# An attention and feed-forward kernel on one core: from sixteen chunks of 288 tokens to nine of 512

## The chip, the cores and the metric

The kernel runs on one core of a Trainium2 chip. The core has a matrix engine (TensorE, PE in the profile; PEld is its loading of weights), a vector engine (VectorE, DVE), a scalar engine (ScalarE, ACT), GpSimd (POOL) and a synchronisation engine (SyncE, SP), which here issues all data transfers. The engines run at the same time, each through its own queue in order, and wait for each other by semaphores. The metric is the device time of one execution in microseconds (us). Three runs of the kernel before took 929.86, 930.31 and 932.52 us; the median is 930.31.

## The reference

```python
# q, k, v: (8, 8, 576, 64) fp32: batch, heads, sequence, head width
window, dilation = 32, 4
scores = q @ k.T / sqrt(64)
rel = pos[:, None] - pos[None, :]
mask_plain = (rel >= 0) & (rel < window)                                        # heads 0 to 3
mask_dil = (rel >= 0) & (rel < window * dilation) & (rel % dilation == 0)       # heads 4 to 7
attn = softmax(where(mask, scores, -1e9))
x = (attn @ v) as (4608 tokens, 512)
out = gelu(x @ w_in) @ w_out              # w_in (512, 2048), w_out (2048, 512)
```

Each query sees at most 32 keys, near ones in the plain heads and every fourth position in the dilated ones. The feed-forward part is two dense products over 4,608 tokens.

## The kernel before, in words

**The products.** Every feed-forward operand is kept as two parts in a short format (`F32R`), a high one and a low one, and a product is made as three: high by high, low weight by high, high weight by low. In the first layer (`ffn_h`, the loop of products at L506) a block `f` of 128 of the 2,048 hidden units takes 4 blocks of inputs by 3, so 12 products; in the second layer (`ffn_o`, L520) each of 4 output blocks `d` takes 16 blocks `f` by 3. That is 16 x 12 + 4 x 16 x 3 = 384 products for one chunk of tokens. Each product has 128 x 128 weights, loaded by an instruction of its own, and streams the chunk's tokens as its columns.

**The chunks.** A chunk is half a batch element: 288 tokens, 16 chunks, 16 x 384 = 6,144 products of 288 columns. After a first-layer block, ACT applies gelu (L510) and makes the high part (L513), and DVE subtracts to get the low one (L515). All of the first layer of a chunk stands before its second layer. The second layer goes output block by output block, and each result is copied (L188, L186) and stored (L545).

**The attention.** The four pairs of heads of a chunk are worked in blocks of 32 queries by 64 keys. Scores (L338) and weighted sums (L458, in the first two chunks L442) are fp32 products on parts of the matrix engine. A chunk has 9 blocks a plain head and 12 or 8 a dilated one, so 84 or 68 products of each kind. Between them DVE adds masks and takes the extreme (L350, L365, L370), ACT does the exponentials (L377), DVE or POOL normalises (L398 to L407), DVE turns the blocks (L417, L422), and ACT and DVE split the result into the two parts of x (L492, L495).

**The weights.** They come as fp64 bit patterns (two 32-bit words a number) and are split into the two parts on the chip: DVE operations at L206 to L231 and L241, one ACT copy at L218. For some, a second load shifted by two bytes (`mid`, L198) saves one DVE operation. After this first stage the weights stay in the core's memory.

**What sets the order.** The first stage (chunks 0 and 1 whole, the attention of chunk 2, all weights) is ordered by a small planner, `Plan`: each job names its steps with an engine and an assumed cost, the buffers it takes from named rings, and a rank; the planner always takes the job that can start first. From chunk 2 on the order is a table: attention steps of chunk c stand at fixed places among the products of chunk c - 1 (`A_SC` for scores, `A_X` for weighted sums, and others). Every engine then does its instructions strictly in the order in which they were recorded, the transfers on SP too.

## Time and profile before

| what | before |
|---|---|
| time, median of 3 runs | 930.31 us (929.86 to 932.52) |
| span of the profiled execution, first to last instruction | 927.7 us |
| instructions in the span | 26,396 |
| PE busy | 900.7 us, 97% |
| DVE, ACT, POOL busy | 492.9, 425.4, 13.1 us |
| mean granted clock of the matrix engine | 1.000 |

For the profiled execution the trace holds its span alone; the median of the runs is 2.6 us above it, and that difference is used as what lies around a span. A group of the profile names the line, the engine, the operation, the tile written and the tiles read, the shape, the count, the busy time, the mean duration in ns, and the idle time ahead of it with what ended it. In the chain of waits a row is the start, the length, the engine, the tile and the line. In the timeline a row is the start, the length to the end of the last instruction merged in it, and the instructions. An fp32 product appears as two records; some records of products are missing.

### The profile page before, as it was taken

The numbers are of one execution on the slowest core, as the hardware profiler recorded it, in microseconds if no ns is written. First come the engines' busy times: TensorE is split into PE (matmuls) and PEld (weight loads), VectorE is DVE, ScalarE is ACT, GpSimd is POOL, SyncE is SP. The second block draws the span as 40 slices with busy tenths as digits, with TensorE's granted clock in tenths as the row PEclk, the third lists the DMA queues.
The fourth block names the chain that finished last, engine by engine and source line by source line (L and its number), as shares of the span: only waits on it lengthen the run. The fifth ranks groups of instructions, "written<-read, shape, count | busy, mean of one in ns | idle before, by whom it ended". The sixth has DMA issues, their size and how long they took to land.

```text
span 927.7 us, 26396 instructions
## 1 busy us (share of the span) xinstructions
PE 900.7 (97%) x11120; PEld 887.8 (96%) x11120; DVE 492.9 (53%) x1815; ACT 425.4 (46%) x1365; POOL 13.1 (1%) x39
## 2 busy tenths in 40 slices
PE   3699999999999999999999999999999999999998
PEld 2599999999999999999999999999999999999998
DVE  7899984454625447353463635436363454635420
ACT  4645443624536245353635437254463624536240
POOL 1400000000000000000000000000000000000000
PEclk9999999999999999999999999999999999999999
DMA  9986334013030210303013030211303012020000
GB/s 326 401 318 232 114 107 151 28 38 115 20 133 17 76 61 27 126 24 116 14 39 114 31 122 19 77 58 37 116 20 116 19 50 103 27 82 7 21 1 26
DMA packets 34838, 81.90 MB, mean 88 GB/s; under 512 B 3872, under 2 KB 12064, under 8 KB 34720
## 3 DMA queue, kind: packets, MB, share of 16 engines
q1 hardware_dynamic: 34720, 80.22, 25.3%
q8 instruction: 87, 1.43, 0.7%
q14 instruction: 31, 0.25, 0.1%
HBM read 70.77 MB, written 9.44 MB: 86 GB/s over the span
## 4 chain that ended last, share of the span: by engine, by line
PE 94%; DMA 3%; DVE 1%; POOL 1%; SPq 0%; issue 0%; POOLq 0%; ACT 0%; DVEq 0%
PE ps_o L520 44%; PE ps_h L506 44%; PE px_a L458 3%; PE ps_a L338 2%; DMA raw_w<-w_out 1%; POOL sm L404 1%; DMA raw_w<-w_in 1%; DMA v_sb<-v_d 1%; DMA v_all<-v_d 0%; PE px L458 0%; DVE cv L208 0%; DVE raw_w L225 0%; DVE x L495 0%; DVE sm L365 0%; DVE cv L206 0%
## 5 line engine op out<-in xcount | busy, mean ns | idle before, releaser
L520 PE MATMUL ps_o<-g,wout 128*128 128x288 f32 x3072 | 418.1, 295 | 0.2 <-DVE x L495 0.2
L520 PEld LDWEIGHTS ps_o<-g,wout 128*128 128x128 f32 x3072 | 409.5, 188 | 1.2 <-DVE x L495 0.5
L506 PE MATMUL ps_h<-xh,win 128*128 128x288 f32 x1920 | 387.1, 297 | 0.0
L506 PEld LDWEIGHTS ps_h<-xh,win 128*128 128x128 f32 x1920 | 308.5, 188 | 1.9 <-issue 0.2
L506 PE MATMUL ps_h<-xl,win 128*128 128x288 f32 x960 | 284.0, 296 | 0.0
L515 DVE TENSOR_TENSOR g<-gf,g 128x288 fp32r<-128x288 f32 x256 | 117.1, 457 | 256.3 <-ACT g L513 256.2
L510 ACT ACTIVATE gf<-ps_h 128x288 f32<-128x288 f32 x256 | 105.4, 412 | 282.7 <-PE ps_h L506 282.7
L506 PEld LDWEIGHTS ps_h<-xl,win 128*128 128x128 f32 x960 | 180.8, 188 | 0.0
L513 ACT CAST g<-gf 128x288 fp32r<-128x288 f32 x256 | 111.0, 434 | 7.9
L377 ACT ACTIVATE sm<-sm,st 128x64 f32<-128x64 f32 (+2 forms) x328 | 109.4, 335 | 10.3 <-DVE st L370 9.4
L492 ACT CAST xh<-px_a 128x256 fp32r<-128x256 f32 (+2 forms) x78 | 27.5, 388 | 123.9 <-PE px_a L458 104.3
L422 DVE STREAM_TRANSPOSE turned<-sm 32x128 f32<-32x128 f32 (+2 forms) x248 | 77.5, 313 | 6.2
L188 DVE COPY o_sb<-ps_o 128x288 f32<-128x288 f32 x59 | 26.8, 456 | 79.9 <-PE ps_o L520 78.1
L377 ACT ACTIVATION_READ_ACCUMULATOR sm<-sm,st 128x1 f32 (+2 forms) x328 | 61.2, 187 | 0.0
L495 DVE TENSOR_TENSOR xl<-px_a,xh 128x256 fp32r<-128x256 f32 (+2 forms) x78 | 28.6, 395 | 39.9 <-ACT xh L492 39.8
L350 DVE CUSTOM_DVE_ANT_0 sm<-ps_a,masks 128x64 f32<-128x64 f32 (+1 forms) x284 | 48.2, 218 | 0.6
L417 DVE STREAM_TRANSPOSE turned<-sm 128x256 f32<-128x256 f32 (+2 forms) x90 | 38.9, 432 | 4.4 <-POOL sm L404 1.4
L407 DVE TENSOR_TENSOR sm<-sm,st 128x256 f32<-128x256 f32 (+2 forms) x86 | 35.3, 411 | 2.7
L458 PEld LDWEIGHTS px_a<-turned,v_all 64*64 64x64 f32 x1960 | 30.5, 135 | 2.8 <-issue 2.8
L458 PE MATMUL px_a<-turned,v_all 64*64 64x32 f32 (+1 forms) x1960 | 32.3, 218 | 0.0
L398 DVE TENSOR_SCALAR st<-st 128x4 f32<-128x4 f32 (+2 forms) x90 | 14.4, 160 | 31.5 <-ACT sm L377 30.4
L506 PE MATMUL ps_h<-x,win 128*128 128x288 f32 x192 | 28.1, 295 | 0.0
(46 smaller groups left out, 366.1 us busy)
## 6 DMA issues: line engine op xcount, KB each, us to landing
v_all<-v_p SPq DMA_DIRECT2D x28, 384.0 KB, 4.6
v_all<-v_d SPq DMA_DIRECT2D x28, 384.0 KB, 6.0
raw_qk<-qk_p SPq DMA_DIRECT2D x32, 304.0 KB, 5.1
outT<-o_sb SPq DMA_DIRECT2D x64, 144.0 KB, 1.7
raw_w<-w_in SPq DMA_DIRECT2D x16, 512.0 KB, 6.2
raw_w<-w_out SPq DMA_DIRECT2D x16, 512.0 KB, 6.7
raw_qk<-qk_w SPq DMA_DIRECT2D x16, 384.0 KB, 3.8
mid_w<-w_in SPq DMA_DIRECT2D x9, 511.5 KB, 6.5
```

The lines of the kernel that those rows point to most:

```text
L350: nc.vector.tensor_tensor_reduce(out=s.sm[rs, i], in0=s.sc[h][rs, cols], in1=mask_of(s, u), scale=-SCALE, scalar=3.0e38, op0=ALU.add, op1= ...
L377: nc.scalar.activation(t, t, AF.Exp, bias=s.st[rs, 0, i:i + 1], scale=-1.0, accum_out=s.st[rs, 1, i:i + 1])
L407: nc.vector.tensor_mul(t, t, st.unsqueeze(2).broadcast_to((rs.stop - rs.start, 2 * (u1 - u0), 2 * KB)))
L417: nc.vector.transpose(s.t[rs, i].rearrange("p i j b -> p (i j b)"), s.sm[rs, i].rearrange("p i k -> p (i k)"))
L422: nc.vector.transpose(s.t[32 * to:32 * to + 32, i, r % 2], s.sm[32 * r:32 * r + 32, i, j * KB:(j + 1) * KB])
L458: nc.tensor.matmul(px[h * D:(h + 1) * D, r - r0, u * KB:u * KB + b], s.v[rows, u, j, h * D:(h + 1) * D], s.t[rows, 2 * u + h, j, 0:b], sta ...
L495: nc.vector.tensor_sub(l, y, h)
L506: nc.tensor.matmul(ps, wins[f][:, t, cc * P:(cc + 1) * P], xx, start=(n == 0), stop=(n == 3 * NC - 1))
L510: nc.scalar.activation(gf, ps, AF.Gelu)
L513: nc.scalar.copy(g[:, 0], gf)
L515: nc.vector.tensor_sub(g[:, 1], gf, g[:, 0])
L520: nc.tensor.matmul(ps, wouts[f][:, t, d * P:(d + 1) * P], gs[f][:, u], start=(f == 0 and n == 0), stop=(f == NF - 1 and n == 2))
```

## The change

- A chunk is now 512 tokens: the first 512 of each batch element make chunks 0 to 7, the last 64 of all eight make chunk 8. So 9 x 384 = 3,456 products of 512 columns.
- A chunk's products stand in four phases: first layer of blocks 0 to 7, second layer of these (block by block, all four output blocks in turn), first layer of blocks 8 to 15, second layer of these (output block by output block). The eight accumulator banks are one tile: banks 0 to 3 hold the second layer's sums, banks 4 and 5 the first layer's, and attention borrows 0 to 3 for scores and 4 to 7 for weighted sums.
- From chunk 1 on the next chunk's attention comes in two visits: all scores after the second first-layer block, all weighted sums nine products into the last phase. Chunk 8's dilated heads have queries with 96 keys each and a third visit.
- Scores and masks of a pair are handled by one DVE operation over both heads and one for the extreme. Normalising, turning and splitting are one operation each of 512 columns, and four more turns.
- The first stage holds chunk 0's feed-forward part and the attention of chunks 0 and 1. Their masks are added by TensorE: an identity times the masks starts each accumulation (L296). Chunk 1's probabilities are normalised on ACT and turned on TensorE (L399), and its weighted sums (L413) take 64 keys at once.
- The two layers' weights of a block are loaded together (1 MB), split by operations of 1,024 columns and kept in one ring of 19 tiles, which also takes queries, keys and values. Output copies are on ACT.
- The planner's costs, ranks and the order of first loads are new.

```diff
+N = 512
+NCH = B + 1
+NW_SPARE = 3
+TWICE = (1, 2, 4, 7, 11, 12, 15)
-    wpool = ctx.enter_context(tc.tile_pool(name="wpool", bufs=1))
-    wo = ctx.enter_context(tc.tile_pool(name="wo", bufs=NF + 2))
+    wpool = ctx.enter_context(tc.tile_pool(name="wpool", bufs=NF + NW_SPARE))
+    xg = ctx.enter_context(tc.tile_pool(name="xg", bufs=12))
...
+    def w_split(s, f, cols):
+        low, top, t = s["raw"][:, cols, 0], s["raw"][:, cols, 1], spare["t"][:, cols]
...
+        if f in TWICE:
+            nc.vector.tensor_scalar(low, s["mid"][:, cols], 0x01FFFFFF, None, op0=ALU.bitwise_and)
+        else:
+            nc.vector.tensor_scalar(low, low, 9, None, op0=ALU.logical_shift_right)
+            yield {"DVE": two}
+            nc.vector.scalar_tensor_tensor(low, top, 23, low, op0=ALU.logical_shift_left, op1=ALU.bitwise_or)
...
+        if s.c < 2:
+            for h in range(2):
+                nc.tensor.matmul(s.sc[:, h, s.at:s.at + 2 * P], diag,
+                                 maskr[:, 0 if s.plain else NU:NU if s.plain else 2 * NU].rearrange("p u k -> p (u k)"),
+                                 start=True, stop=False)
...
+    def ffn_h(c, f, gs):
+        yield {"PE": 2.73}
+        bank = ps[:, 4 + f % 2]
...
+    A_SC, A_LOW, A_E, A_N, A_X, A_QK, A_V = 2, 2.5, 8.5, 10.5, 24.75, 26.5, 3
...
+    half = NF // 2
+    for c in range(1, NCH):
+        gs = {}
+        base = 2 * NF * c
+        for f in range(half):
+            at_once(ffn_h(c, f, gs))
+            upto(base + f + 1)
+        for f in range(half):
+            for d in range(NC):
+                ffn_o(d, f, gs)
+                upto(base + half + f + (d + 1) / 4)
+        for f in range(half, NF):
+            at_once(ffn_h(c, f, gs))
+            upto(base + half + f + 1)
+        for d in range(NC):
+            for f in range(half, NF):
+                ffn_o(d, f, gs)
+                upto(base + 3 * half + 2 * d + (f - half + 1) / 4)
+            at_once(store(c, d, 2 if c == LAST and d == NC - 1 else 1))
```

The order on PE before, from the second layer of a late chunk into the first layer of the next one; `ps_o` and `ps_h` are the accumulators of the two layers, `px_a` the weighted sums:

```order
L520 MATMUL ps_o<-g,wout 128x288 x135
L458 MATMUL px_a<-turned,v_all 64x32 x84
L520 MATMUL ps_o<-g,wout 128x288 x57
L506 MATMUL ps_h<-xh,win_121 128x288 x2
L506 MATMUL ps_h<-xl,win_121 128x288
L506 MATMUL ps_h<-xh,win_121 128x288 x2
```

And now, one whole middle chunk; all accumulators are `ps`, L501 and L516 are the two layers, L310 the scores, L459 the weighted sums:

```order
L501 MATMUL ps<-x,weight 128x512 x24
L310 MATMUL ps<-raw_qk 32x64 x128
L501 MATMUL ps<-x,weight 128x512 x72
L516 MATMUL ps<-g,weight 128x512 x96
L501 MATMUL ps<-x,weight 128x512 x96
L516 MATMUL ps<-g,weight 128x512 x9
L459 MATMUL ps<-turned,v_sb 64x32 x128
L516 MATMUL ps<-g,weight 128x512 x87
```

The products have 512 columns in place of 288, a visit has 128 attention products in place of 84 or 68, and there are two visits in 384 products of the longer kind.

The order on SP before, from the last weight to the first loads for the attention of chunk 3, by way of the stores of chunks 0 and 1:

```order
L194 DMA raw_w<-w_out 128x1024
L545 DMA outT<-o_sb 128x288 x3
L286 DMA v_all<-v_p 128x768
L545 DMA outT<-o_sb 128x288
L286 DMA v_all<-v_p 128x768
L286 DMA v_all<-v_d 128x768
L545 DMA outT<-o_sb 128x288
L286 DMA v_all<-v_d 128x768
L545 DMA outT<-o_sb 128x288 x3
L279 DMA raw_qk<-qk_p 128x608 x2
```

And now, from the last weight to the loads for the attention of chunk 2 (with what each waits for), by way of the four stores of chunk 0:

```order
L194 DMA raw_w_1369<-w 128x2048 [waits DMAHW4_49,DVE_49]
L534 DMA outT<-o_sb_1555 128x512 [waits Activation_49]
L534 DMA outT<-o_sb_1557 128x512 [waits DVE_49]
L534 DMA outT<-o_sb_1559 128x512 [waits DMAHW5_49,Activation_49]
L534 DMA outT<-o_sb_1563 128x512 [waits DMAHW6_49,Activation_49]
L260 DMA raw_qk_1657<-qk 128x1024 [waits DMAHW7_49]
L260 DMA raw_qk_1657<-qk 128x1024 [waits DMAHW0_49]
L260 DMA raw_qk_1660<-qk 128x1024 [waits DMAHW1_49]
L260 DMA raw_qk_1660<-qk 128x1024 [waits DMAHW2_49]
L272 DMA v_sb_1829<-v 128x2048 [waits DMAHW3_49]
```

Before, the values for chunk 2's weighted sums were woven among the stores and chunk 2's scores were long done; now all four stores stand ahead of the queries and keys for chunk 2's scores.

## The prediction

> **What bounds the kernel now.** I read the head of the page first, then the chain of waits in order of time, then the matrix engine's timeline near its first product.

> ```profile
> span 927.7 us, 26396 instructions
> PE 900.7 (97%) x11120; PEld 887.8 (96%) x11120; DVE 492.9 (53%) x1815; ACT 425.4 (46%) x1365; POOL 13.1 (1%) x39
> PE   3699999999999999999999999999999999999998
> DVE  7899984454625447353463635436363454635420
> PE 94%; DMA 3%; DVE 1%; POOL 1%; SPq 0%; issue 0%; POOLq 0%; ACT 0%; DVEq 0%
> ```

> PE is busy from the third slice to the last and is 94% of the chain that ends last. Nothing else comes near, so a change is worth what it does to PE's queue, plus what it does to the first 150 us, where PE still waits. The chain shows both:

> ```profile
> 127.65 6.36 PE ps_o L520 x48
> 134.85 4.50 DMA v_all<-v_d
> 139.49 0.90 PE px L458 x48
> ...
> 151.62 6.37 PE ps_h L506 x48
> ...
> 329.93 1.90 PE ps_a L338 x115
> 331.83 14.54 PE ps_h L506 x108
> 346.37 17.88 PE ps_o L520 x135
> 364.25 2.58 PE px_a L458 x168
> 366.83 7.73 PE ps_o L520 x57
> 374.56 6.38 PE ps_h L506 x48
> 380.94 1.58 PE ps_a L338 x97
> ...
> 419.71 2.10 PE px_a L458 x136
> ...
> 899.02 25.43 PE ps_o L520 x192
> ```

> A feed-forward product of 288 columns takes a slot of 25.43/192 = 0.1324 us. The two attention visits of a chunk take 1.90 + 2.58 us (84 products each) or 1.58 + 2.10 us (68 each), so 22.9 ns a score product and 30.8 ns a weighted-sum product; an fp32 product is recorded twice, and some score records are missing, so I count products by the program. After a visit PE needs a little longer: 57 products in 7.73 us are 0.18 us over 57 slots, 108 in 14.54 are 0.24 over, so 0.42 us for a chunk's two visits.

> Check on before: chunk 2's first product is at 151.62; 14 chunks of 384 slots are 711.8 us, 13 chunks' visits 52.7, their restarts 5.5: 921.6. The last copy, quoted below, starts at 924.47. The missing 2.9 us are the four chunks whose visits are split further. The sum can be trusted to half a per cent.

> **The products' length, the largest term.** Both kernels do 4,608 tokens, so the columns streamed are the same: 16 x 384 = 6,144 products of 288 before, 9 x 384 = 3,456 of 512 after. Only what a product costs beside its columns can be saved. The trace has no 512-column product, but it has the 288-column one at two speeds:

> ```profile
> 36.16 0.85 PE L506 MATMUL ps_h<-xh,win 128*128 128x288 f32 x2
> 36.81 0.44 PE L506 MATMUL ps_h<-xl,win 128*128 128x288 f32 x1
> 37.05 0.68 PE L506 MATMUL ps_h<-xh,win 128*128 128x288 f32 x2
> 37.53 0.44 PE L506 MATMUL ps_h<-xl,win 128*128 128x288 f32 x1
> 37.77 0.68 PE L506 MATMUL ps_h<-xh,win 128*128 128x288 f32 x2
> ...
> 41.24 0.43 PE L506 MATMUL ps_h<-xh,win 128*128 128x288 f32 x2
> 41.51 0.29 PE L506 MATMUL ps_h<-xl,win 128*128 128x288 f32 x1
> 41.65 0.43 PE L506 MATMUL ps_h<-xh,win 128*128 128x288 f32 x2
> ```

> Three products are 0.72 us apart at 37 us (37.05 to 37.77: 240 ns each) and 0.40 us at 41 us, the steady 132.4. I take the first as half speed. If columns are all of the 240 ns, they are 120 at full speed, and 12.4 ns are fixed: a 512-column slot is 12.4 + 120 x 512/288 = 225.7 ns. If the fixed part is there at both speeds, it is 2 x 132.4 - 240 = 24.8 ns, columns are 107.6, and the slot is 216.1. If nothing is fixed, it is 235.4. A third row-based hint: recorded attention products follow each other after 11.3 ns (1.90 us / 168) to 15.4 ns (2.58 / 168; 2.10 / 136 is 15.4 too, with 16 of its 68 products half as wide). That is what PE spends on an instruction however narrow; as the fixed part it gives 223 to 227. So I take **225.7**, with 216.1 and 235.4 as ends. All 3,456: 780.0 us against 813.5 before, a gain of 33.5.

> [...]

> Could weight loading, one per product, set the slot? These rows say no:

> ```profile
> L506 PEld LDWEIGHTS ps_h<-xh,win 128*128 128x128 f32 x1920 | 308.5, 188 | 1.9 <-issue 0.2
> L458 PEld LDWEIGHTS px_a<-turned,v_all 64*64 64x64 f32 x1960 | 30.5, 135 | 2.8 <-issue 2.8
> ```

> Four quadrants share the weighted sums, so one quadrant turns round in 4 x 15.4 = 61.6 ns; 64 more weight columns cost 188 - 135 = 53 ns, so a full load could recur every 115 ns, inside 132.4, and more so inside 225.7.

> **Attention visits.** A visit now has 128 products, whatever the chunk: 128 x 22.9 + 128 x 30.8 = 6.87 us, and 0.42 for restarts: 7.3. Six such chunks (2 to 7) are 43.8. The last chunk has 64 score products of 96 columns (bounds: the 64-column price, and 1.5 times it; 1.8 us taken) beside 64 plain ones (1.5), and 64 + 192 weighted sums (7.9); with three restarts 11.8. Together 55.6, against 58.2 + 2.9 for 13 chunks before. The scores wait for nothing new: their banks 0 to 3 are the accumulators, whose last copy is queued on ACT right at the chunk's end, and the visit stands behind 24 products (5.4 us). The weighted sums use banks 4 to 7 nine products (2.0 us) after the last first-layer product; its gelu has to be out by then, about 0.7 us of ACT (412 ns for 288 columns, below). The exps, 32 x 0.34 us with their table loads, stand in a phase of 96 second-layer products (21.7 us) in which ACT has no gelu.

> ```profile
> 8.37 0.35 ACT L377 ACTIVATE sm<-sm,st 96x64 f32<-96x64 f32 x1 [6.35 <-DVE st L370]
> 8.71 0.33 ACT L377 ACTIVATE sm<-sm,st 96x64 f32<-96x64 f32 x1
> L510 ACT ACTIVATE gf<-ps_h 128x288 f32<-128x288 f32 x256 | 105.4, 412 | 282.7 <-PE ps_h L506 282.7
> L164 POOL TENSOR_SCALAR_AFFINE_SELECT masks<-masks 32x64 f32<-32x64 f32 (+1 forms) x11 | 2.5, 232 | 0.6
> ```

> **The first stage.** Before, it takes 151.6 us for 576 tokens (101.7 us of slots). After, it holds 512 tokens (86.7) and the attention of chunks 0 and 1. When can PE begin? The masks must stand before the first score (12 selects of 232 ns, copies, the casts on ACT), so I put the first exp a microsecond after the 8.37 of now; chunk 0's 32 exps at 0.34 us end at 20.3; the last pair's normalising, turn, weighted sum and split follow: 27. From there PE has 86.7 of products, chunk 1's 128 + 128 products (6.9), eight mask products (at most 0.13 each: 1.1), 16 transposes (0.5 to 4, by the 30.8 ns product and the half-speed 240; 2 taken), and cold slots (2): 126, if never short of weights. DVE feeds it:

> ```profile
> 61.74 0.41 DVE L206 TENSOR_SCALAR cv<-raw_w 128x512 uint32<-128x512 uint32 x1
> 62.07 0.67 DVE L241 SCALAR_TENSOR_TENSOR wout<-raw_w 128x512 fp32r<-128x512 uint32 x1
> 62.67 0.68 DVE L208 SCALAR_TENSOR_TENSOR cv<-raw_w,cv 128x512 uint32<-128x512 uint32 x1
> 63.28 0.44 DVE L515 TENSOR_TENSOR g<-gf,g 128x288 fp32r<-128x288 f32 x1
> 63.65 0.41 DVE L212 TENSOR_SCALAR raw_w<-cv 128x512 uint32<-128x512 uint32 x1
> ```

> Start to start, a one-input operation is 0.33 us at 512 columns, a two-input one 0.60. At 1,024 they are at most twice that. A weight loaded once has three of each (5.6 us), one loaded twice three and two (4.4): 9 x 5.6 + 7 x 4.4 = 81. Chunk 0's attention on DVE, about seven operations a pair, is at most 14, chunk 1's, with its turning on PE and normalising on ACT, 8, the 16 subtractions 11: 114, from about 8 on, so 122 with no idle time; the last weight's two jobs and its gelu (7) come after it: 129. Two estimates three apart; I take **129**, 125 to 136.

> At its end a wait moves. SP's order has the four output stores ahead of chunk 2's query and key loads, and the last of them waits for ACT's third copy (three copies at 0.6 us). The loads go out about 2.4 us after the last product, 2 MB of them; now v_all held PE for 4.5 us in such a place. The scores stand 5.4 us behind: **3 us** of wait (0 to 5).

> **The end** is a copy and a store as now, so 927.7 - 924.47 = 3.2 us:

> ```profile
> 924.47 0.46 DVE L188 COPY o_sb<-ps_o 128x288 f32<-128x288 f32 x1 [5.89 <-PE ps_o L520]
> ```

> Sum: 129 + 3 + 8 x 86.7 (693.3) + 55.6 + 3.2 = 884.1 as a span. The profiled execution's span is 927.7 and the median of the runs 930.31, so 2.6 us lie around it: **886 us**, 44 below: 33.5 from the products, the rest from the first stage and fewer visits.

> **The rivals.** *A, columns cost less and the fixed part more* (24.8 ns): 9.6 ns off each of 3,456 slots, 853 us. For it: the two speeds read that way. Against: instructions as narrow as 16 columns need only 15.4 ns. *B, nothing is fixed*: the products stay at 813.5 and the time is 919. For it: no product of another width in the trace; against: the half-speed row would then be 265, not 240. *C, PE waits in each chunk*: three spare slots for keys, queries and values where there were separate pools, so loads start when the slot before is free; 7 chunks at the 4.5 us of v_all, 918. Against: a load has 5 to 20 us of lead. *D, slower: the first stage is paced by its loads.* Raw weight, shifted copy and result share one ring of 19 slots, so towards the end a 1 MB load waits for the weight before the last to be split. If load (6.2 to 6.9 us for half as much in a busy queue), split (5.6) and copy ran in series, a weight would take 14 us, and the stage over 220. It decides from 44/16 = 2.8 us of lateness per weight on: above that the kernel is slower, about 935 to 980. Against: DVE now has full slices while loads land, and only the last third of the weights is short of slots.

> ```profile
> raw_w<-w_in SPq DMA_DIRECT2D x16, 512.0 KB, 6.2
> mid_w<-w_out SPq DMA_DIRECT2D x9, 511.5 KB, 6.9
> ```

> **How the numbers follow.** Forecast 0.70 (its own range 874 to 898), A 0.10, B 0.07, C 0.08, D 0.05. The range 852 to 908 holds the forecast, half of A and the lighter half of C, and leaves out about 0.18. Faster by over 0.3% (about the least that a measurement can tell from no change): all but D and a bad C, 0.93; same 0.02; slower 0.05.

> **What would show it.** The 512-column slot in a stretch without visits: near 226 right, 216 A, 235 B. Chunk 2's scores should start near 137 us behind a query and key load. In the later chunks the chain should be PE alone, at about 94 us a chunk; named waits there are C. In the first stage, DVE idle on weight loads after 60 us is D, and makes the forecast wrong whatever the slot is.

## The result, and the profile after

The changed kernel takes **954.12 us** (median of 4 runs, 950.3 to 954.67) against 930.35 us (929.86 to 932.52) for the kernel before on the same chip. The ratio is 1.0244, 95% interval 1.0222 to 1.0265. It is slower, where 886 us was forecast and slower had been given 0.05.

The head of the page of the changed kernel, PE's granted clock in 40 slices, the queue that carries PE's instructions (count, MB, share of time) and the chain's shares by engine:

```profile
span 951.8 us, 19064 instructions
PE 889.0 (93%) x8408; PEld 733.4 (77%) x8408; DVE 359.5 (38%) x608; ACT 373.6 (39%) x1017; POOL 9.6 (1%) x48
PEclk9579999999999999999999999999999999979999
q8 instruction: 66, 1.08, 0.5%
PE 88%; issue 4%; ACT 3%; DVE 3%; DMA 1%; POOL 0%; SPq 0%; POOLq 0%; ACTq 0%; DVEq 0%
```

PE is still the chain, but two things are new in it. There is 4% of "issue", time in which PE waited for nothing that the profile shows; before it was 0%. And the clock is not whole everywhere: its mean is 0.964, before 1.000. The group of the scores has much of the idle time (the last numbers of the row):

```profile
L310 PE MATMUL ps<-raw_qk 64*32 64x64 f32 (+1 forms) x2304 | 31.3, 239 | 17.4 <-issue 15.2
```

and PE's waits for "issue" have all of it (the total in us, how often, the longest):

```profile
PE ps L310 <- issue: 15.2, 7, 3.4
PE ps L459 <- issue: 7.7, 6, 1.4
PE ps L429 <- issue: 6.7, 2, 4.0
PE ps L451 <- issue: 5.6, 3, 2.3
```

All of it lies in the attention products: the scores (L310), the weighted sums of later chunks (L459, and L451 in the last), the weighted sums of chunk 0 (L429). Here are the two visits of one chunk in the chain, in order of time (start, length, what; rows left out are marked):

```profile
265.04 2.64 PE ps L310 x168
267.68 2.05 issue
269.74 0.56 PE ps L310 x20
270.30 17.93 PE ps L501 x72
...
309.99 21.76 PE ps L501 x96
...
333.79 3.38 PE ps L459 x218
337.17 1.31 issue
```

Long runs of 96 products take 21.76 us, so a 512-column slot is 226.7 ns. Each visit is cut in two: PE runs short products for some 2.6 to 3.4 us, stops for 2.05 or 1.31 us, and runs the rest. The 72 products behind the scores take 17.93 us, where 72 slots are 16.32: 1.6 us more. The windows of the same places (length, busy time of PE, PEld, DVE, ACT and POOL, granted clock, DMA share, GB/s) give the reason; the last row is the place behind a later stop, of 2.07 us in chunk 5's scores:

```profile
264.90:270.20 5.30, 3.25 (x257) 2.82 (x256) 0.69 (x1) 1.22 (x2) 0.00 (x0) 0.97 0.50 173
270.30:273.60 3.30, 3.30 (x9) 2.63 (x10) 0.00 (x0) 0.00 (x0) 0.00 (x0) 0.55 0.12 42
278.00:288.00 10.00, 10.00 (x46) 8.29 (x45) 6.63 (x10) 4.28 (x7) 0.00 (x0) 1.00 0.00 0
468.90:472.30 3.40, 3.40 (x15) 2.81 (x16) 0.00 (x0) 0.45 (x1) 0.00 (x0) 1.00 0.17 67
```

After this stop PE's granted clock is half for 3.41 us (0.55 over the second window), so the stop costs its own 2.05 us and then the 1.6 us of the 72 products. That is not so behind every stop: in the trace's record of the clock, half clock follows six of the twelve stops in chunks 2 to 7 (two of the scores', four of the sums') and not the others, as the last row shows. In this record every stretch of half clock within the span lasts 3.41 us or two, three or six times that (6.83, 10.24, 20.48), and the starts lie on one grid of 3.41 us (235.73, 269.86, 437.12, 536.10, 635.09). Whether a stop's place on this grid decides was not tested.

What did PE wait for? The instruction queue moved 66 packets, 1.08 MB; PE carries 2 x 8408 = 16,816 instructions. That is 16.4 KB a packet and 255 instructions a packet. Before it was 87 packets for 2 x 11,120: 256 each. So, by the counts of these two traces, PE's program comes in pieces of 256 instructions. The trace gives the start and length of each packet; around this visit:

```
piece of PE's instructions, 16 KB: starts 266.93, takes 1.29 us
PE's last product before the stop: 267.47; the first one after it: 269.73
piece of PE's instructions, 16 KB: starts 270.85, takes 1.34 us
```

A feed-forward product is two instructions (load and product) in 226.7 ns, so 256 last 29 us. A score product is four, as the two records of an fp32 product each have their load, in 22 ns: 256 last 1.4 us, and a visit of 128 products is 512 instructions. From the landing (268.22) to PE's next product are another 1.5 us. A first theory follows: **the visit is longer than the store of instructions at hand; PE runs dry, stops about 2 us, and the clock falls.** In PE's timeline, which has all 256 records of this visit where the chain has fewer, the first part of this visit is

```profile
264.97 2.71 PE L310 MATMUL ps<-raw_qk 64*32 64x64 f32 x236
```

so the stop came after 236 records, 472 instructions; in the sums, after 218 records, 436. Before, a visit had at most 84 products, 336 instructions.

But these counts are no lengths that the store allows. Each record of a product goes with one of a load, so twice the number of records is a place in PE's program. Counted so from the first record, all 18 stops for instructions of this run, from 20.98 us to 836.54 us, lie at a multiple of 256 plus 190 to 172 (falling by 2 a chunk, as if each chunk had two instructions that the profile does not count). So each of these stops comes where a piece ends. The last chunk's sums show it: 192 products behind 64 others, the second and third stop 128 records, one piece, after the one before.

```profile
828.09 1.07 PE L451 MATMUL ps<-turned,v_wide 32*64 32x32 f32 x85
830.77 1.47 PE L451 MATMUL ps<-turned,v_wide 32*64 32x32 f32 x128 [1.61 <-issue]
834.50 2.04 PE L451 MATMUL ps<-turned,v_wide 32*64 32x32 f32 x128 [2.26 <-issue]
```

In all 18, PE goes on 1.2 to 1.6 us after a piece has landed. A visit of 512 instructions holds two piece ends, here 216 and 472 instructions into the scores and 180 and 436 into the sums: the first passes, the second stops PE. A middle chunk is 768 + 1,024 = 1,792 instructions, seven pieces, so every chunk meets the ends at nearly the same places. From one piece end to PE's going on at the next were 3.2 to 3.7 us in chunks 3 to 8. The theory, put more exactly, and drawn from these rows alone: a piece that PE uses up sooner than the next one can come leaves it without instructions.

Against the forecast's span of 884.1, the 951.8 us hold 67.7 more. Read from the trace: the first stage ends at 152.4 instead of 129 (+23.4); chunk 2's first visit, beyond the 3 us allowed (+3.5); slots of 226.7 in place of 225.7 (+3.0); the visits, with their stops, beyond their forecast length in the scores of chunks 3 to 7 (+10.4), in the weighted sums (+9.7) and in the last chunk (+4.9); the products behind the visits beyond their slots and the forecast restarts, which is the half clock (+12.2); the end (+0.5). The sum is 67.6.

### The profile page after: what moved, and what is told of

It is laid out like the page before. It is cut to its first block, busy times and chain, and to the rows that moved or that the text cites. A ratio compares the mean times of both kernels' runs of the same rounds, so it can differ in the third digit from the quotient of the medians.

```text
span 951.8 us, 19064 instructions
## 1 busy us (share of the span) xinstructions
PE 889.0 (93%) x8408; PEld 733.4 (77%) x8408; DVE 359.5 (38%) x608; ACT 373.6 (39%) x1017; POOL 9.6 (1%) x48
## 3 DMA queue, kind: packets, MB, share of 16 engines
q8 instruction: 66, 1.08, 0.5%
## 4 chain that ended last, share of the span: by engine, by line
PE 88%; issue 4%; ACT 3%; DVE 3%; DMA 1%; POOL 0%; SPq 0%; POOLq 0%; ACTq 0%; DVEq 0%
PE ps L516 41%; PE ps L501 40%; PE ps L459 3%; PE ps L310 3%; ACT sm L355 1%; DMA raw_qk<-qk 1%; PE ps L429 1%; PE ps L451 1%; DMA raw_w<-w 0%; PE ps L296 0%; DVE raw_w L221 0%; DVE weight L227 0%; DVE st L324 0%; DVE x L490 0%; ACT x L487 0%
## 5 line engine op out<-in xcount | busy, mean ns | idle before, releaser
L501 PE MATMUL ps<-x,weight 128*128 128x512 f32 x1728 | 408.3, 396 | 7.6 <-ACT weight L232 7.6
L516 PE MATMUL ps<-g,weight 128*128 128x512 f32 x1728 | 408.5, 396 | 0.0
L501 PEld LDWEIGHTS ps<-x,weight 128*128 128x128 f32 x1728 | 329.8, 191 | 78.3 <-ACT weight L232 8.5
L516 PEld LDWEIGHTS ps<-g,weight 128*128 128x128 f32 x1728 | 329.9, 192 | 69.8
L511 DVE TENSOR_TENSOR g<-gf,g 128x512 fp32r<-128x512 f32 x144 | 99.6, 692 | 432.7 <-ACT g L509 432.7
L506 ACT ACTIVATE gf<-ps 128x512 f32<-128x512 f32 x144 | 86.1, 598 | 336.1 <-PE ps L501 335.9
L509 ACT CAST g<-gf 128x512 fp32r<-128x512 f32 x144 | 89.4, 621 | 4.6
L355 ACT ACTIVATE sm<-sm,st 128x64 f32<-128x64 f32 (+1 forms) x224 | 74.9, 337 | 0.1
L185 ACT COPY o_sb<-ps 128x512 f32<-128x512 f32 (+1 forms) x35 | 20.3, 581 | 124.5 <-PE ps L516 123.7
L310 PE MATMUL ps<-raw_qk 64*32 64x64 f32 (+1 forms) x2304 | 31.3, 239 | 17.4 <-issue 15.2
L392 DVE STREAM_TRANSPOSE turned<-sm 32x256 f32<-32x256 f32 x104 | 45.4, 436 | 2.0
L310 PEld LDWEIGHTS ps<-raw_qk 64*32 64x32 f32 x2304 | 26.5, 111 | 23.6 <-issue 21.6
L355 ACT ACTIVATION_READ_ACCUMULATOR sm<-sm,st 128x1 f32 x224 | 42.1, 188 | 0.0
L459 PE MATMUL ps<-turned,v_sb 64*64 64x32 f32 x1664 | 28.1, 223 | 7.7 <-issue 7.7
L459 PEld LDWEIGHTS ps<-turned,v_sb 64*64 64x64 f32 x1664 | 26.7, 138 | 10.7 <-issue 10.7
## 6 DMA issues: line engine op xcount, KB each, us to landing
raw_qk<-qk SPq DMA_DIRECT2D x32, 512.0 KB, 6.0
```

Source lines behind the costliest of these rows:

```text
L310: nc.tensor.matmul(s.sc[32 * r:32 * r + 32, h, c0:c0 + s.nk], x[:, q0:q0 + 32], x[:, k0:k0 + s.nk], start=s.c > 1, stop=s.c > 1 or u == NU ...
L355: nc.scalar.activation(t, s.sc[:, i // NU, at:at + 2 * KB] if s.c < 2 else t, AF.Exp, bias=s.st[:, 0, i:i + 1], scale=SCALE if s.c < 2 els ...
L392: nc.vector.transpose(s.t[32 * to:32 * to + 32, :, r % 2], s.all[32 * r:32 * r + 32, :, j * KB:(j + 1) * KB])
L459: nc.tensor.matmul(px(r)[h * D:(h + 1) * D, u * KB:(u + 1) * KB], s.v[rows, u, j, h * D:(h + 1) * D], s.t[rows, h * NU + slot(s, u), j], s ...
L501: nc.tensor.matmul(bank, weights[f][:, t, cc * P:(cc + 1) * P], x[:, xx], start=n == 0, stop=n == 3 * NC - 1)
L506: nc.scalar.activation(gf, bank, AF.Gelu)
```

## Experiments

Rivals to the first theory: the visits are slow because the products are slow (a wait on banks, or dearer narrow products), so that cutting them up changes nothing; or transfers, not length, hold the instructions back; or the order that the planner chose is at fault in the first stage.

**Visits of 64 products.** Pairs 2 and 3 of each chunk are moved 36 first-layer products (scores) or 24 second-layer products (weighted sums) behind pairs 0 and 1; in the last chunk each of pairs 2 and 3 has its own place for the sums.

```diff
-            add(c, A_SC if not wide else 8.25, 1, scores(s[p], bank))
+            second = 0 if late or p < 2 else 3
+            add(c, A_SC + second if not wide else 8.25, 1, scores(s[p], bank))
...
-            add(c, A_X, 6, av(s[p], px[0]))
+            a_x = A_X + (0 if p < 2 else 2 * (p - 1) if late else 2)
+            add(c, a_x, 6, av(s[p], px[0]))
```

> The changed kernel with each attention visit of 128 products cut into two of 64, with 36 first-layer or 24 second-layer products between them; the last chunk's 192 weighted sums of three key blocks into two of 96. Same products, same banks. Theory 1, PE runs out of instructions: in the changed kernel a visit stops after about 236 or 218 recorded products (each with a weight load, so some 440 to 470 instructions) for about 2 us that the profile calls issue, while instructions come in pieces of 16 KB, 256 of them; a visit of 64 products (256 instructions) should not stop. Then the scores take about 1.4 us and the weighted sums about 2.0 a visit as the last chunk's 64-product visits already do, the clock stays at 0.99 or more, and about 10 + 10 + 5 + 14 us go: 912 to 920. Theory 2, the visit waits for something in the fourth pair (its banks, its operands): the waits stay, about 950. [...]

Measured: 917.04 us (916.43 to 917.44), ratio 0.9855 (0.9841 to 0.987). This one edit turns the slower kernel into one that is 1.5% faster than before. PE's timeline at the same place in this run:

```profile
264.68 1.48 PE L310 MATMUL ps<-raw_qk 64*32 64x64 f32 x128
266.09 8.46 PE L501 MATMUL ps<-x,weight 128*128 128x512 f32 x36
```

The window behind it, where the clock is now 1.00:

```profile
270.30:273.60 3.30, 3.30 (x16) 2.74 (x15) 2.43 (x4) 1.32 (x3) 0.00 (x0) 1.00 0.00 0
```

The page's clock in 40 slices:

```profile
PEclk9988999999999999999999999999999999999999
```

And the one stop for instructions that is left after the first stage:

```profile
801.86 2.08 PE L451 MATMUL ps<-turned,v_wide 32*64 32x32 f32 x189
805.63 0.30 PE L451 MATMUL ps<-turned,v_wide 32*64 32x32 f32 x3 [1.68 <-issue]
```

Sixty-four score products take 266.09 - 264.68 = 1.41 us and 64 sums 2.00: 22.0 and 31.3 ns a product, with no stop, and the clock stays whole (1.00 in this window). From the 384th feed-forward product to the last, the run takes 757.9 us against 795.3: 37.4 us less, where the visits' excess and the half clock above add up to 37.2. The products were not slow; the pauses were. Two more readings: the stop that is left is in the last chunk, in a visit of 96 products, 384 instructions, that holds two piece ends, at 122 and 378, and it comes at the second; and in the first stage the clock is higher here than in the changed kernel (slices 2 to 4: 9, 8, 8 against 5, 7, 9), though the 384th product is at 153.1 us here and 152.4 there. So the clock alone is not what makes the first stage long.

**Visits of 96 and 32.** The same edit with `p < 3` in place of `p < 2` outside the last chunk: 96 products are 384 instructions, fewer than the 436 after which PE was seen to stop.

> As the run before it, but the visits are 96 products (three pairs) and 32, not 64 and 64. Theory 1 with a store of some 450 instructions: 96 products are 384 instructions, so no stop, 912 to 921. If the store is only about 256 instructions, or if a visit stops after some 2 us whatever the count, the 96-product visits stop too, scores take over 2.6 us and sums over 3.5 us, and the time is about 930 to 940. Theory 2 (fourth pair): waits move to the 32-product visits, about 950.

Measured: 942.41 us (941.71 to 942.76), ratio 1.0128 (1.0113 to 1.0143). It lies between the expected numbers, for a reason that none of them had. From chunk 3 on the 96-product scores and sums run without a stop, in 2.06 and 2.93 us. That is not a store of 384 instructions: at these places the second piece end, 472 or 436 instructions from the visit's start, lies beyond the visit, and in the last chunk a visit of 96 products stops, as in the run before. It does rule out that a visit stops after some time: the sums run 2.93 us through where the changed kernel's scores stopped after 2.7. But the last pair's scores now wait for something else. PE's waits:

```profile
PE ps L310 <- DVE sm L341: 16.0, 6, 2.7
```

The chain through one of the six:

```profile
270.78 0.69 DVE g L511
271.47 0.61 DVE sm L341
272.13 1.06 PE ps L310 x61
```

The window behind it, at half clock:

```profile
272.50:275.80 3.30, 3.30 (x50) 2.59 (x37) 0.29 (x1) 0.00 (x0) 0.00 (x0) 0.51 0.00 0
```

Pair 3's scores go to the two banks that pair 2's scores lie in, and DVE reads those (L341) only after it has made the low part of a gelu (L511), for which it waits on ACT. PE stands 2.7 us, and again the clock is half for the 3.3 us behind. Each of six chunks loses some 2.7 us in the wait and 1.4 in the clock: 25 us, and 917 + 25 = 942. So the run fits the theory, and shows that a stop for DVE (2.7 us), which has nothing to do with instructions, was followed by half clock as well (0.51); here half clock follows all six, which are one chunk, 99.0 us, apart: 29 steps of the grid of 3.41 us. In the 64-product form the pairs of one bank move together.

**The cause put into the kernel before.** Each score product of chunks 3 to 15 is issued twice, with the same result; a visit then has 168 or 136 products.

```diff
-                    nc.tensor.matmul(...)
+                    for _ in range(2 if s.c > 2 else 1):
+                        nc.tensor.matmul(...)
```

> The kernel before with every score product of chunks 3 to 15 issued twice, one right after the other, into the same place (the second overwrites the first): visits of 168 or 136 products, 672 or 544 instructions, in place of 84 or 68. Theory 1: the kernel before, which never stopped, now stops in each of these 13 visits for about 2 us after some 220 to 240 recorded products, and the clock drops after some of them: 13 x (1.74 + 2.1 + 0.5 to 1.5) more, 983 to 1000. [...]

Measured: 1003.16 us (two runs, 999.74 and 1006.57), ratio 1.0781 (1.0734 to 1.0829), a little above what was expected. The kernel that had 0% of issue stops in the visits, which now look like those of the changed one; one visit in PE's timeline, and the products behind it in the chain:

```profile
346.69 2.45 PE L339 MATMUL ps_a<-raw_qk 64*32 64x64 f32 x175
351.04 2.16 PE L339 MATMUL ps_a<-raw_qk 64*32 64x64 f32 x128 [1.90 <-issue]
354.77 0.74 PE L339 MATMUL ps_a<-raw_qk 64*32 64x64 f32 x33 [1.57 <-issue]
355.51 16.13 PE ps_h L507 x108
```

Twice in a visit of 672 instructions PE stops (1.90 and 1.57 us), the second time one piece (128 records) after the first, and the 108 products behind it take 16.13 us where they took 14.54. The added products, about 1,000 at 22.9 ns, would have cost 23 us; 73 came. None of the new chunk size, banks and loads is needed for it, only more short products in one burst. The first stop comes after 128 to 257 records in the 13 visits, 256 to 514 instructions, always where a piece ends: no count from the visit's start tells where PE stops.

**Chunk 2's loads ahead of the stores.** Its query and key loads are issued with the last weight's split instead of behind the four stores of chunk 0.

```diff
+    for i in range(NPAIR):
+        dma(("load", 2, i), load(xs[2][i]), ["w"] if i % 2 == 0 else [],
+            [("wsplit", NF - 1, len(parts(NF - 1)) - 1)] if i else [("first", ("wsplit", NF - 1, 0))])
...
-            add(c, ..., 0, load(s[p]))
+            if n > 2:
+                add(c, ..., 0, load(s[p]))
```

> The changed kernel with chunk 2's four query and key loads issued ahead of the four output stores at the end of the first stage; nothing moves on the other engines. In the changed kernel the first scores visit takes 8.8 us, of which 2.2 are waits for these loads and 3.4 an instruction wait behind them, and starts 0.7 late. If the loads' place is the cause, the visit falls to the 5 us of the later ones and the time by 3 to 6 us, 948 to 951. If the loads land late for another reason, no change: 954.

Measured: 946.37 us (944.69 to 949.2), ratio 1.0177 (1.015 to 1.0203), 7.7 under the changed kernel; a little more than expected. Chunk 2's scores as the changed kernel has them:

```profile
158.61 0.85 PE L310 MATMUL ps<-raw_qk 64*32 64x64 f32 x64 [0.42 <-DMA raw_qk<-qk]
160.38 0.86 PE L310 MATMUL ps<-raw_qk 64*32 64x64 f32 x64 [0.92 <-DMA raw_qk<-qk]
167.04 0.41 PE L310 MATMUL ps<-raw_qk 64*32 64x64 f32 x19 [3.41 <-issue]
```

The loads themselves held PE for only 2.2 us; the stop for instructions behind them is 3.41, longer than in the later visits, with the transfer engines 0.95 busy from 162.9 to 167.1. With the loads out of the way that stop is 1.51 us.

**Both edits**, 64-product visits and early loads:

> Both: visits of 64 products and chunk 2's query and key loads ahead of the stores. If the 7.7 us that the loads' place alone gave and the 37.1 us of the split visits are separate losses, 909. If most of the former was the instruction wait of the first visit and the clock drop behind it, which the split already removes (its first visit takes 1.94 us against 1.41 for the later ones and starts 0.9 late), only 1.5 us are left to gain: 914 to 916.

Measured: 914.2 us (913.47 to 915.77), ratio 0.983 (0.9816 to 0.9845). The loads are worth 2.8 us once the visits are short; most of the 7.7 belonged to the stops and the clock behind them. Most of what is left lies in the first stage, where the next runs start from.

**The first stage: fewer transfers beside chunk 0's weighted sums.** In the changed kernel the first feed-forward product starts at 40.9 us, forecast at 27. The timelines of ACT (chunk 0's last exponential), of PE, and of DVE (its first step that needs PE's sums):

```profile
23.27 0.37 ACT L355 ACTIVATE sm<-ps,st 128x64 f32<-128x64 f32 x1
28.95 1.35 PE L429 MATMUL ps<-turned,v 32*64 32x64 f32 x69 [4.05 <-issue]
35.05 0.64 PE L429 MATMUL ps<-turned,v 32*64 32x64 f32 x22 [2.68 <-issue]
40.91 4.26 PE L501 MATMUL ps<-x,weight 128*128 128x512 f32 x10 [2.08 <-ACT weight L232]
35.80 0.69 DVE L490 TENSOR_TENSOR x<-ps,x 128x512 fp32r<-128x512 f32 x1 [8.84 <-PE ps L429]
```

and the window of the second stop, with clock and DMA share as the third and second numbers from the end:

```profile
30.00:40.00 10.00, 3.99 (x180) 3.39 (x168) 3.29 (x7) 4.09 (x19) 0.00 (x0) 0.50 1.02 417
```

The exponentials end at 23.6 instead of 20.3. Then PE stops twice for instructions, 6.7 us, DVE stands 8.84 us behind it with the first weight's split queued after, and PE's first product waits for that weight. The transfer engines are full (1.02), and the pieces start 6 us apart (20.41, 26.38, 32.49). The edit holds SP, after chunk 0's values, until the first block of x is made: a 4 KB transfer that waits for x stands in SP's queue ahead of the later weights.

```diff
+    def pause():
+        yield {"DMA": 0.1}
+        nc.sync.dma_start(scratch, xs[0][0].x[:, 0, 0:8].bitcast(F32))
...
+        if x == "v2":
+            dma(("pause",), pause(), [], [("x", 0, 0)])
```

> The run before it, with SP held after the first values until the first part of x stands (a transfer of 4 KB that reads it), so that the next 10 MB of weights no longer fill the transfer engines while PE does chunk 0's weighted sums. In the changed kernel PE stops there three times for instructions, 1.9, 4.1 and 2.7 us, and its first feed-forward product starts at 40.9 us. Theory 1 (instructions come late because the same engines are full of loads): the stops shrink to the 1.4 to 2.2 us of a visit, together by 3 to 5 us, and the first product starts at about 36; what the whole time does depends on the weights, which now land later: 905 to 920. If the stops are as long as before, full queues are not their reason.

Measured: 910.02 us (906.4 to 910.34), ratio 0.9771 (0.9746 to 0.9795). In its timeline:

```profile
24.28 0.92 PE L429 MATMUL ps<-turned,v 32*64 32x64 f32 x69 [1.46 <-issue]
28.11 0.64 PE L429 MATMUL ps<-turned,v 32*64 32x64 f32 x22 [0.82 <-issue]
33.96 5.26 PE L501 MATMUL ps<-x,weight 128*128 128x512 f32 x12 [2.08 <-ACT weight L232]
```

and in its windows, where the DMA share from 20 to 30 us was 1.01 in the run before it:

```profile
20.00:30.00 10.00, 5.77 (x298) 4.80 (x298) 6.38 (x17) 6.63 (x41) 0.00 (x0) 0.76 0.24 72
```

Two stops of 1.46 and 0.82 us in place of 4.05 and 2.68 (4.25 and 2.69 in the run that this edit starts from); pieces at 18.06, 21.50 and 25.35, under 4 us apart; the first product 7.5 us sooner. So here PE's stops were longer with the DMA share at 1.01 than with it at 0.24. The 384th product comes 6.8 us sooner (146.0 against 152.8), of which the rest of the run gives back 1.2; the profiled executions stand 5.6 us apart and the medians 4.2.

**The first stage: masks back on DVE.** For chunks 0 and 1 the mask products are left out, and one DVE operation adds the mask and turns the sign, as in later chunks.

```diff
-                nc.tensor.matmul(s.sc[:, h, s.at:s.at + 2 * P], diag, maskr[...], start=True, stop=False)
...
+            m = dil_masks if s.c < 2 and not s.plain else masks[:, k:k + NU]
```

> Split visits and early loads, and the first stage's masks undone: no identity products on TensorE, DVE adds the masks of chunks 0 and 1 as it does in the later chunks (one operation of 512 columns a pair more, less the scaling of the extreme). In the changed kernel the first score waits until 7.0 us for the masks (3.7 in the kernel before). If that wait is on the path, the first feed-forward product starts 2 to 4 us sooner and the time falls by as much; if the path goes by DVE, whose 8 more operations are 5 us, the time grows by up to 4 us; in both cases under 1% of 915.

Measured: 909.92 us (909.08 to 910.37), ratio 0.9781 (0.9766 to 0.9796), 4.3 under its starting point. The masks on TensorE were a loss of 2.6 us in the trace, though not where it was looked for: the first score starts at 4.15 instead of 7.04, but the first feed-forward product is no sooner (41.9 against 41.5). The 384th is 2.6 us sooner, and why it is that much is not settled. After it the profiled run saves another 4.0 us, in the last chunk: the one stop that short visits had left, with the half clock behind it, does not occur:

```profile
797.71 2.11 PE L440 MATMUL ps<-turned,v_wide 32*64 32x32 f32 x192
```

That visit is the same in both programs. But PE's program is 16 records, 32 instructions, shorter ahead of it, so the piece end that lay 378 instructions into it lies at 410, behind its 384. These 4.0 us are luck and not the masks' doing. (The profiled executions stand 6.6 us apart, the medians 4.3.)

**The planner's costs.** Its cost for a pair's sums is set to 2.4 (0.95) and its time of half clock to 58 (38; in the changed kernel's record the last of the early half clock ends at 58.2 us), so that it plans with what was measured.

```diff
-LATE, LATE_PE, COLD = 0.25, 0.55, 38
+LATE, LATE_PE, COLD = 0.25, 0.55, 58
...
-        yield {"PE": 0.95}
+        yield {"PE": 2.4}
```

> Split visits and early loads, with the planner of the first stage told two things that the trace of the changed kernel showed: PE at half speed until 58 us (38 assumed), and 2.4 in place of 0.95 us for a pair's weighted sums in chunk 0 (4.3 with their stops measured, before its own factor of 1.6). If the first stage is late because its order was made for engines that are not so late (ACT's exps of chunk 1 stand ahead of gelus that PE waits for, 71 to 85 us), a few us go: 905 to 912. If it is late because of its work and its instruction stops, no order changes it: 914 to 918.

Measured: 915.48 us (913.65 to 917.02), ratio 0.9841 (0.9824 to 0.9858): no gain over 914.2. Telling the planner these two costs does not make the first stage shorter; that no other order would is not shown.

**Everything together**: 64-product visits, early loads, held transfers, masks on DVE.

> Split visits, early loads, the held transfers and the masks back on DVE, all together. If the held transfers shorten PE's stops for instructions (7 us of them in chunk 0's weighted sums) and the masks on DVE spare chunk 1 DVE's drain of banks, the two gains of some 4 us each add: 905 to 908 us, and waits for issue ahead of the first-stage weighted sums under 3 us. If both only let the same later job (the last weight's split) end earlier, they do not add: 909 to 911.

Measured: **903.38 us** (902.41 to 904.72), ratio 0.9715 (0.9699 to 0.9731), the fastest of all, a little below the expected range. The gains add: the 384th product is at 143.5, 9.3 us sooner, where 6.8 and 2.6 came from each alone. PE's clock on its page:

```profile
PEclk9999999999999999999999999999999999999999
```

## Why the prediction was wrong, step by step

**The products' length: right.** 225.7 ns forecast, 226.7 measured, in every stretch without a visit; the part beside the columns is, with columns estimated from the 240 ns row (213.3 and 120 ns), about 13 ns at 512 columns and 12 at 288. Rival A (216) and rival B (235) are out. The 3,456 products gain 813.5 - 783.4 = 30 us of the forecast 33.5. At half clock, behind the stop at 267.68 (0.55 in the window 270.30 to 273.60), the products start 427 ns apart, which is 240 x 512/288: the reading that the half-speed row is columns alone held.

**Attention visits: wrong, and the step that failed first.** The step was "128 x 22.9 + 128 x 30.8 = 6.87 us, and 0.42 for restarts: 7.3". The price of a product was right: 22.0 and 31.3 ns, 6.82 us a chunk, once a visit has 64. What fell was that a visit of 128 costs 128/84 of one of 84. The price came from bursts of at most 336 instructions, none of which had stopped, and was carried to bursts of 512, which always hold two piece ends. With the stops, scores and sums take about 5.0 and 5.5 us, and the half clock behind them more: some 37 us by the trace, 37.4 by the run that only shortens the visits. That alone turns a gain into a loss: 954 - 917. The forecast's "later chunks PE alone at about 94 us a chunk" would have come true without it: from the 384th product to the last, the prediction has 3 + 693.3 + 55.6 = 751.9 us, and the run with everything together 753.4.

Could the profile of before have told it? It could have told that PE runs short of instructions, though not at what price. This row of its waits was not read:

```profile
PE px L442 <- issue: 9.2, 6, 2.1
```

In its first two chunks the weighted sums already stopped six times, up to 2.1 us, with no releaser; four of these stops lie one piece apart in PE's program. The prediction took PE's 0% of "issue" in the chain for the whole truth.

**The first stage: wrong by 23.4 us** (152.4 for 129). The step "the last pair's normalising, turn, weighted sum and split follow: 27" missed by 13.9: 3.3 of it are exponentials that end later, 6.7 are stops for instructions, and the rest follows on DVE and the first weight's split. Masks on TensorE were priced at "1.1"; taking them off brings the first score 2.9 us and the stage's end 2.6 us forward. From the first product to the 384th it took 111.5 us instead of 102. In that stretch ACT goes twice from gelu to the exponentials of chunk 1 and back, with rows of this kind in the chain of the changed kernel:

```profile
71.26 1.28 ACT L355
72.55 2.47 ACT sm L355 x16
75.04 1.28 ACT L506
```

Two such rounds are 5.1 us each, while the gelus of the first blocks wait. That they are the missing 9.5 us is argued, not tried. The half clock is a second candidate: 17.3 us of this stretch have it in the changed kernel, where the forecast had 2 us for "cold slots", a term for which no row was named and that no run shows by itself, and with all edits none has and the stretch takes 105.6 us; but in the run with held transfers and the masks still on TensorE 11.7 us have it and the stretch takes 112.0, so the runs do not separate the two. With all edits the stage still ends at 143.5, and what of that could be had stays open.

**Chunk 2's loads.** "3 us of wait (0 to 5)" was 2.2 by the trace for the loads and 2.8 by the run with short visits: right. The 3.41 us stop beside them belongs to the visits. **The end** is 3.7 us for the forecast 3.2.

**The rivals.** C said that PE waits in each chunk; it does, but for instructions, not for loads, so its test ("named waits there") found 2.2 us, all in chunk 2's visit. D is out: in the first stage DVE has no wait for a weight's load among its waits, and 152 is far from 220; that the kernel is slower all the same has nothing to do with it. No rival held the mechanism that decided. The chance of 0.05 for slower was read from one rival only, while the forecast rested on a burst length that no row of the trace had. Two sums are slightly off: 884.1 + 2.6 is 886.7, and what the range leaves out by the listed chances is 0.21, not 0.18.

## What to carry to other kernels

A price per instruction is known only up to the longest burst in the trace: before lengthening a burst of short matrix products, count its instructions, loads included, against the piece in which they arrive (here 256: 66 packets for 16,816). Behind the first stage of these runs a burst of at most one piece ran through, with long products between the bursts; one of 384 ran or stopped by where the ends fell; one of 512 stopped in all 12 visits of the changed kernel's chunks 2 to 7. In time, from chunk 3 on in the changed kernel and with short visits: a piece used up in 1.5 to 2.1 us was followed by a stop, one that lasted 5.7 us or more was not. Read the "issue" rows of the waits by line, above all in the stage with full transfer engines, even when the chain shows 0%. When cutting a burst in two, cut it so that the second part does not write a bank that another engine has yet to read (up to 2.7 us of wait in each of six chunks in the run with 96 and 32).

## What was not expected of the hardware

In chunks 2 to 7 of the changed kernel, behind stops of 1.08 to 3.41 us for instructions among short products, PE's granted clock was half for 3.41 us, once for 6.83 (a stop of 2.05 us, then 0.55 in the window of 3.3 us); that was behind 6 of the 12 stops, always on a grid of 3.41 us. In the run with 96 and 32 it was half behind 6 of 6 stops for DVE (2.7 us, then 0.51 in such a window), 99.0 us apart, which is 29 steps of that grid. What else decides whether the clock falls is not shown: other stops of 1.31 to 2.10 us in the changed kernel were followed by the whole clock.
